# ScalarE's queue instead of SyncE's for the loads of float64 weight blocks and the stores of converted weights

## The chip, the cores and the metric

The kernel runs on one core of a Trainium2 chip. The metric is device time in microseconds for one execution. Three runs of the kernel before took 1545.47, 1546.47 and 1552.09 us, so the median is 1546.47 us. The profiled execution, from which all rows below are taken, took 1545.34 us; its span from the first to the last recorded instruction is 1543.5 us, which leaves 1.84 us around the span.

## The reference, cut to what matters

```
# q, k, v: (4, 8, 1152, 64) float32; two MLPs of d_model 512, d_ff 2048, weights float64
q_pool = q.reshape(B, H, S // 2, 2, D).mean(axis=3)          # 576 queries
scores = q_pool @ k.T / sqrt(D)
attn   = exp(scores - max) ; attn /= attn.sum() + 1e-9
x      = (attn @ v)  -> (2304, 512)
h = x @ w_in   ; x   = max(0.01 * h, h) @ w_out              # layer 0 (moe)
h = x @ w_in2  ; out = elu(h) @ w_out2                       # layer 1 (moe2)
```

Everything is computed in float32; the products of the two MLPs and of the attention are split into high and low parts, which is why most copies below come in pairs (a "hi" copy and a "lo" subtraction).

## The kernel before, in words

**Work.** Attention runs over 16 pairs of heads (4 batches, 4 pairs each). After each batch's attention its 576 rows go through the two MLPs; an MLP is 16 slices `f` of 128 hidden columns, each with an "up" product (line 629) and a "down" product (line 667). The MLPs of one batch overlap in time with the attention of the next.

**Weights.** `load_w` (line 311 on) gives slice `f` its two weight tiles `wr` of 128x512 float32, one of `w_in` and one of `w_out`. The first time a slice is used (batch 0 of each layer) the float64 words come from the input and are turned into float32 by `convert`, in blocks of 256 words: two blocks per tile, so 2 layers x 16 slices x 2 tensors x 2 blocks = 128 blocks. A block is a load into the tile `cr` (line 290), two operations on VectorE (lines 293 and 296), two on ScalarE (299 and 301), one on GpSimd (303) and a last one on VectorE that writes half of `wr` (305). `cr` has two buffers (`CB = 2`), so the load of a block has to wait until the block two before has been read by all of 293, 296, 299, 301 and 303. A finished `wr` tile is stored to DRAM as `w` (line 328, 64 stores), and the three later batches load it from there (line 323, 192 loads). From `wr`, `psplit` makes the high part on ScalarE and the low part on GpSimd (lines 261 and 267) into `wi` and `wo`; `wr` has four buffers, `wi` three and `wo` six.

**Order.** The kernel writes down each engine's instructions in an order of its own. Every operation is handed to `prog.add` with an engine, a cost in nanoseconds and a rank (a place in the wanted order); `schedule` then plays the program through with these costs: on each engine the operation with the lowest rank among those whose inputs are ready starts next. An operation's results count as ready after its end plus a latency by engine (2500 ns behind a DMA on SP). Operations are emitted in the order of the planned starts, and the engines execute them in that order, each waiting for its own inputs. All DMAs, these loads and stores too, are operations of the engine "SP" with a cost of 60 ns, and are issued from SyncE's queue, in one row with the loads of q, k and v (line 349), of `w` (323) and the stores of the output (712). A matmul of the MLPs enters the plan with 123 ns (369 for a group of three).

Of the kernel before, what the change touches and what calls it, by code (L numbers as in the profile page):

```python
# [11 lines left out]
U32 = mybir.dt.uint32  # L12
# [24 lines left out]
class Program:  # L37
# [8 lines left out]
               "PE PE": 5}  # L46

    def __init__(self):
        self.ops, self.tags = [], {}

    def buf(self, tag, bufs, make):
        used = self.tags.setdefault(tag, [])
# [1 line left out]
        used.append(b)  # L54
        return b

    def add(self, engine, cost, rank, fn, w=(), r=()):

        me = len(self.ops)
        deps, starts, frees = set(), set(), []  # L60

        def hits(accesses, part):
            return [o for o, p in accesses if p is None or part is None or p == part]

        for x in r:
            b, part = x if isinstance(x, tuple) else (x, None)
            deps.update(hits(b.writers, part))
            b.readers.append((me, part))
        for x in w:
            b, part = x if isinstance(x, tuple) else (x, None)  # L70
            deps.update(hits(b.writers, part))
            deps.update(hits(b.readers, part))
            if b.first is None:
                b.first = me
            if b.prev is not None:
                frees.append(b.prev)
            if b.before is not None:
                starts.add(b.before)
            b.writers.append((me, part))
        deps.discard(me)  # L80
        self.ops.append((engine, cost, rank, fn, deps, starts, frees))

    def schedule(self):
        ops, n = self.ops, len(self.ops)
        out = [[] for _ in range(n)]
        need = [0] * n
        for i, (_, _, _, _, deps, starts, frees) in enumerate(ops):
            d = set(deps)
            for b in frees:
                d.update(o for o, _ in b.writers + b.readers)  # L90
            d.discard(i)
            starts = {b.first for b in starts}
            for o in d:
                out[o].append((i, True))
            for o in starts - d:
                out[o].append((i, False))
            need[i] = len(d | starts)
        ready = [0.0] * n
        start = [None] * n
        idle, waiting, open_ = {}, {}, {}  # L100
        for o in ops:
            idle[o[0]] = 0.0
            waiting[o[0]], open_[o[0]] = [], []
        for i in range(n):
            if not need[i]:
                heapq.heappush(waiting[ops[i][0]], (0.0, i))
        times = [0.0]
        left = n
        while left:
            now = heapq.heappop(times)  # L110
            while times and times[0] <= now:
                heapq.heappop(times)
            again = True
            while again:
                again = False
                for e in idle:
                    while waiting[e] and waiting[e][0][0] <= now:
                        i = heapq.heappop(waiting[e])[1]
                        heapq.heappush(open_[e], (ops[i][2], i))
                    if idle[e] > now or not open_[e]:  # L120
                        continue
                    i = open_[e][0][1]
                    if e != "SP" and any(
                            t < now + self.PATIENCE * ops[i][1] and ops[o][2] < ops[i][2] - self.GAP
                            for t, o in waiting[e]):
                        continue
                    heapq.heappop(open_[e])
                    start[i] = now
                    left -= 1
                    end = idle[e] = now + ops[i][1]  # L130
                    heapq.heappush(times, end)
                    again = True
                    for o, done in out[i]:
                        e2 = ops[o][0]
                        if not done:
                            t = now
                        elif e2 == "PE" and e not in ("PE", "SP"):
                            t = end + 200
                        else:
                            t = end + self.LATENCY.get(e + " " + e2, self.LATENCY[e])  # L140
                        ready[o] = max(ready[o], t)
                        need[o] -= 1
                        if not need[o]:
                            heapq.heappush(waiting[e2], (ready[o], o))
                            heapq.heappush(times, ready[o])
        return start
# [8 lines left out]
def kernel(  # L155
# [19 lines left out]
    nc = tc.nc  # L175
    V, A, G, PE = nc.vector, nc.scalar, nc.gpsimd, nc.tensor
# [66 lines left out]
    def sb(tag, shape, dt=F32, bufs=1):  # L243
        return prog.buf(tag, bufs, lambda: sp.tile(shape, dt, tag=tag, name=tag, bufs=bufs))
# [26 lines left out]
    def convert(rank, dst, src):  # L271

        for n in range(0, 512, CW):
            r = sb("cr", [128, CW, 2], U32, CB)
            t = sb("ct", [128, CW], U32, CB)  # L280
            mag = sb("cm", [128, CW], F32, CB)

            def load(n=n, r=r):
                rv = r.ap.rearrange("p n t -> p (n t)")
                if len(src.shape) == 3:
                    k0, kn = n // src.shape[2], CW // src.shape[2]
                    rv, sv = rv.rearrange("p (c n) -> p c n", c=kn), src[:, k0:k0 + kn, :]
                else:
                    sv = src[:, n:n + CW]
                nc.sync.dma_start(out=rv, in_=sv.bitcast(U32))  # L290

            prog.add("SP", 60, rank - 1, load, w=[r])
            prog.add("DVE", dve(CW, True), rank, lambda r=r, t=t: V.tensor_scalar(  # L293
                out=t.ap, in0=r[:, :, 1], scalar1=3, scalar2=0x3FFFFFF8,
                op0=ALU.logical_shift_left, op1=ALU.bitwise_and), w=[t], r=[(r, 1)])
            prog.add("DVE", dve(CW), rank, lambda r=r, t=t: V.scalar_tensor_tensor(  # L296
                out=t.ap, in0=r[:, :, 1], scalar=0xC0000000, in1=t.ap,
                op0=ALU.bitwise_and, op1=ALU.bitwise_or), w=[t], r=[(r, 1), t])
            prog.add("ACT", act(CW, sbuf=True), rank, lambda r=r: A.activation(
                out=r[:, :, 0], in_=r[:, :, 0], func=ACTF.Copy, scale=2.0 ** -29), w=[(r, 0)], r=[(r, 0)])  # L300
            prog.add("ACT", act(CW, sbuf=True), rank, lambda r=r, mag=mag: A.activation(
                out=mag.ap, in_=r[:, :, 1].bitcast(F32), func=ACTF.Abs), w=[mag], r=[(r, 1)])
            prog.add("POOL", pool(CW), rank, lambda t=t, r=r: G.tensor_tensor(  # L303
                out=t.ap, in0=t.ap, in1=r[:, :, 0], op=ALU.add), w=[t], r=[t, (r, 0)])
            prog.add("DVE", dve(CW), rank, lambda n=n, t=t, mag=mag: V.scalar_tensor_tensor(  # L305
                out=dst[:, n:n + CW], in0=mag.ap, scalar=MIN_HI, in1=t.ap.bitcast(F32),
                op0=ALU.is_ge, op1=ALU.mult), w=[(dst, n)], r=[t, mag])
# [3 lines left out]
    def load_w(rank, layer, w_in, w_out, f):  # L311

        src = (w_in[:, f * 128:(f + 1) * 128].rearrange("(c p) f -> p c f", p=128),
               w_out[f * 128:(f + 1) * 128, :])
        rs = [sb("wr", [128, 512], F32, WRB) for _ in range(2)]
        for i, r in enumerate(rs):
            if w_in.dtype == F32:
                view = (lambda r=r: r.ap.rearrange("p (c n) -> p c n", c=DC)) if i == 0 else lambda r=r: r.ap
# [6 lines left out]
            else:  # L325
                convert(rank - CLEAD, r, src[i])
                kp = kept[layer, f, i] = Buf(lambda i=i: dram.tile([128, 512], F32, name=f"w{layer}_{f}_{i}"))
                prog.add("SP", 60, rank, lambda r=r, kp=kp: nc.sync.dma_start(out=kp.ap, in_=r.ap), w=[kp], r=[r])
        wi = sb("wi", [128, 2, DC, 128], F32R, WIB)
        wo = sb("wo", [128, 2, DM], F32R, WOB)  # L330
        psplit(rank - 0.5, WH, WL, lambda: wi[:, 0].rearrange("p c n -> p (c n)"),
               lambda: wi[:, 1].rearrange("p c n -> p (c n)"), lambda: rs[0].ap, 512, (wi, 0), [rs[0]])
        psplit(rank - 0.5, WH, WL, lambda: wo[:, 0], lambda: wo[:, 1], lambda: rs[1].ap, 512, (wo, 0), [rs[1]])
        return wi, wo


# [258 lines left out]
    def mlp(at, span, b, layer, xin, w_in, w_out, tags):  # L595
# [22 lines left out]
        def up(f):  # L618
# [4 lines left out]
            for hf in range(2):  # L623
# [7 lines left out]
                            start=(c == 0 and a == 0 and e == 0), stop=(c == DC - 1 and a == 1))  # L631

                for c in range(DC):
                    prog.add("PE", 3 * 123, rank + step * hf / 2, lambda h=h, c=c, cols=cols: mm(h, c, cols),
                             w=[h], r=[wi, (xs[c], hf), (xs[c], 2 + hf)])
                rk = rank + step * hf / 2 - HURRY
                t = sb("t1", [128, HB], F32, T1B)
# [19 lines left out]
        def down(fc):  # L657
            for hf in range(2):
                for d in range(DC):
# [10 lines left out]
                                stop=(f % FC == FC - 1 and a == 1))  # L670

                    for f in fs:
                        prog.add("PE", 3 * 123, rank, lambda f=f, mm=mm: mm(f), w=[y],
                                 r=[w[f][1], (g[f], hf), (g[f], 2 + hf)])
                    a_ = acc[d]
                    if fc == 0:
# [92 lines left out]
```

## Time and profile before

| what | kernel before |
|---|---|
| median of 3 runs (lowest, highest) | 1546.47 us (1545.47, 1552.09) |
| the profiled execution | 1545.34 us |
| its span | 1543.5 us |
| busy in the span: TensorE, VectorE | 1414.5 us (92%), 1011.4 us (66%) |
| busy in the span: ScalarE, GpSimd | 1065.9 us (69%), 830.3 us (54%) |
| mean share of the 16 DMA engines' time, queue of all tensor DMAs | 28.0% |
| chain that ended last: TensorE, VectorE, ScalarE, DMA | 64%, 21%, 6%, 3% |

In the rows, PE is TensorE, PEld its weight loads, DVE VectorE, ACT ScalarE, POOL GpSimd, and SPq the queue of SyncE. L290 is line 290 of the kernel. A row of waits names an engine that stood idle, the tile and line it was about to start, and the instruction whose end released it. The busy share is an average over stages with different limits, so the stages are looked at one by one.

### The profile page before, as it was taken

How to read it: one execution, taken by the hardware profiler on the slowest of the kernel's cores; microseconds unless marked ns; L12 is line 12 of the kernel's file. 1: busy time of each engine (PE TensorE's matmuls, PEld its weight loads, DVE VectorE, ACT ScalarE, POOL GpSimd, SP SyncE). 2: the span in 40 equal slices, each digit the busy share in tenths (PEclk: the TensorE clock that was granted, in tenths of full speed). 3: DMA queues.
4: the chain of work that ended last, by engine and by line, in shares of the span. 5: the costliest groups of instructions: out<-in, count | busy, mean ns of one | idle time of the engine just before them, and what ended most of it. 6: DMA issues, size and time to landing. Idle time of an engine off the chain costs nothing.

```text
span 1543.5 us, 28953 instructions
## 1 busy us (share of the span) xinstructions
PE 1414.5 (92%) x10288; PEld 1365.2 (88%) x10288; DVE 1011.4 (66%) x2273; ACT 1065.9 (69%) x2901; POOL 830.3 (54%) x840
## 2 busy tenths in 40 slices
PE   5878889888888898999999999999999999899997
PEld 4777788888878887999999999899999998899897
DVE  6999889899998998556565556645665554124222
ACT  6989878776678787676668776676667763443553
POOL 5443255765766667254555556254554445466662
PEclk9999999999999999999999999999999999999999
DMA  4332123343334443222222222222221121322221
GB/s 138 99 115 87 40 75 123 121 130 125 126 118 144 130 143 120 74 71 73 67 69 86 79 78 63 74 76 66 71 67 59 55 56 56 93 76 82 69 82 39
DMA packets 82642, 135.59 MB, mean 88 GB/s; under 512 B 8512, under 2 KB 26944, under 8 KB 82496
## 3 DMA queue, kind: packets, MB, share of 16 engines
q1 hardware_dynamic: 82496, 133.73, 28.0%
q8 instruction: 81, 1.33, 0.4%
q14 instruction: 65, 0.53, 0.1%
HBM read 112.20 MB, written 21.50 MB: 87 GB/s over the span
## 4 chain that ended last, share of the span: by engine, by line
PE 64%; DVE 21%; ACT 6%; issue 3%; DMA 3%; POOL 2%; SPq 0%; ACTq 0%; POOLq 0%; DVEq 0%
PE h L667 17%; PE h L629 16%; PE s L452 8%; PE o L496 7%; PE t L475 5%; DVE m L457 3%; PE s L629 3%; DVE ct L293 3%; DVE wr L305 3%; DVE ct L296 3%; DVE pt L267 2%; PE s L667 2%; PE t L373 2%; PE t L629 2%; PE t L667 2%
## 5 line engine op out<-in xcount | busy, mean ns | idle before, releaser
L667 PE MATMUL h<-g,wo 128*128 128x288 f32 x2544 | 437.1, 302 | 17.5 <-DVE t L650 7.9
L629 PE MATMUL h<-xs,wi 128*128 128x288 f32 x2520 | 429.2, 305 | 22.9 <-DVE t L650 14.2
L629 PEld LDWEIGHTS h<-xs,wi 128*128 128x128 f32 x2520 | 362.5, 190 | 32.5 <-DVE t L650 20.0
L667 PEld LDWEIGHTS h<-g,wo 128*128 128x128 f32 x2544 | 367.1, 188 | 23.8 <-DVE t L650 9.6
L457 DVE TENSOR_REDUCE m<-s 128x1 f32<-128x384 f32 x432 | 232.2, 550 | 74.4 <-PE s L452 71.6
L261 ACT ACTIVATE pt<-t 128x384 fp32r<-128x384 f32 (+1 forms) x416 | 184.0, 457 | 115.2 <-PE t L475 108.3
L463 ACT ACTIVATE p<-s,m 128x384 f32<-128x384 f32 x432 | 249.5, 588 | 18.3 <-DVE m L459 18.0
L267 DVE TENSOR_TENSOR pt<-t,pt 128x384 fp32r<-128x384 f32 (+1 forms) x416 | 206.8, 509 | 73.3 <-ACT pt L261 71.7
L267 POOL TENSOR_TENSOR g<-t,g 128x288 fp32r<-128x288 f32 x256 | 211.1, 831 | 79.9 <-ACT g L261 75.5
L267 POOL TENSOR_TENSOR wo<-wr,wo 128x512 fp32r<-128x512 f32 x128 | 166.4, 1304 | 137.5 <-ACT wo L261 134.3
L452 PE MATMUL s<-kT,qT 128*128 128x384 f32 x768 | 197.0, 354 | 25.4 <-ACT p L463 24.5
L267 POOL TENSOR_TENSOR wi<-wr,wi 128x512 fp32r<-128x512 f32 x128 | 167.6, 1309 | 91.9 <-ACT wi L261 79.3
L496 PE MATMUL o<-pt,vn 128*128 128x256 f32 (+1 forms) x1152 | 192.5, 303 | 5.5 <-DVE pt L267 3.6
L475 PE MATMUL t<-ident,p 128*128 128x128 f32 x1116 | 181.6, 277 | 12.4 <-DVE pt L267 11.7
L496 PEld LDWEIGHTS o<-pt,vn 128*128 128x128 f32 x1152 | 165.5, 190 | 10.6 <-DVE pt L267 10.2
L475 PEld LDWEIGHTS t<-ident,p 128*128 128x128 f32 x1116 | 139.4, 142 | 22.1 <-DVE pt L267 12.3
L452 PEld LDWEIGHTS s<-kT,qT 128*128 128x128 f32 x768 | 125.5, 192 | 32.2 <-ACT p L463 31.0
L303 POOL TENSOR_TENSOR ct<-ct,cr 128x256 uint32<-128x256 uint32 x128 | 98.8, 774 | 96.7 <-DVE ct L296 29.8
L261 ACT ACTIVATE g<-t 128x288 fp32r<-128x288 f32 x256 | 112.2, 445 | 49.0 <-DVE t L650 28.4
L267 POOL TENSOR_TENSOR vn<-raw,vn 128x576 fp32r<-128x576 f32 x32 | 46.4, 1449 | 174.4 <-ACT vn L261 174.4
L261 ACT ACTIVATE wo<-wr 128x512 fp32r<-128x512 f32 x128 | 80.6, 630 | 78.9 <-PE h L667 47.5
L680 DVE TENSOR_TENSOR acc<-h,acc 128x288 f32<-128x288 f32 x158 | 71.1, 452 | 67.2 <-PE h L667 66.1
(106 smaller groups left out, 2080.0 us busy)
## 6 DMA issues: line engine op xcount, KB each, us to landing
wr<-w SPq DMA_DIRECT2D x192, 256.0 KB, 2.6
cr<-in_moe_w_in_dram SPq DMA_DIRECT2D x64, 256.0 KB, 2.7
cr<-in_moe_w_out_dram SPq DMA_DIRECT2D x64, 256.0 KB, 2.7
w<-wr SPq DMA_DIRECT2D x64, 256.0 KB, 2.4
raw<-in_k_dram SPq DMA_DIRECT2D x32, 288.0 KB, 3.0
raw<-in_v_dram SPq DMA_DIRECT2D x32, 288.0 KB, 3.1
raw<-in_q_dram SPq DMA_DIRECT2D x32, 256.0 KB, 2.9
out_dram<-cr SPq DMA_DIRECT2D x16, 256.0 KB, 2.1
```

Of the source, the lines that this page charges most:

```text
L261: prog.add("ACT", act(n, sbuf=not psum), rank, lambda: A.activation(out=hi(), in_=src(), func=ACTF.Copy), w=[w], r=r)
L267: lambda: eng.tensor_tensor(out=lo(), in0=src(), in1=f32(hi()), op=ALU.subtract),
L293: prog.add("DVE", dve(CW, True), rank, lambda r=r, t=t: V.tensor_scalar(out=t.ap, in0=r[:, :, 1], scalar1=3, scalar2=0x3FFFFFF8, op0=ALU.l ...
L303: prog.add("POOL", pool(CW), rank, lambda t=t, r=r: G.tensor_tensor(out=t.ap, in0=t.ap, in1=r[:, :, 0], op=ALU.add), w=[t], r=[t, (r, 0)])
L452: PE.matmul(out=st[:, 0:384], lhsT=qa(a), rhs=kT[:, 384 * c:384 * c + 384], start=(i == 0), stop=(i == len(seq) - 1))
L457: prog.add("DVE", dve(384), rank - LR, lambda st=st, c=c: V.tensor_reduce(out=m[:, c:c + 1], in_=st[:, 0:384], axis=AX.X, op=ALU.max), w=[ ...
L463: prog.add("ACT", act(384, True), rank - LE, lambda c=c: A.activation(out=p[:, 384 * c:384 * c + 384], in_=banks[c][:, 0:384], func=ACTF.E ...
L475: PE.transpose(out=t[:, i, :], in_=p[:, (3 * c + i) * 128:(3 * c + i + 1) * 128], identity=ident)
L496: PE.matmul(out=o[:, 0:n], lhsT=vn[:, c, :], rhs=pt[th][:, a, c % 3, :], start=(c == 3 * ORDER[0] and a == 0), stop=(c == 3 * ORDER[2] + 2 ...
L629: PE.matmul(out=h[:, 0:HB], lhsT=wi[:, a, c, :], rhs=xs[c][:, e, cols], start=(c == 0 and a == 0 and e == 0), stop=(c == DC - 1 and a == 1))
L667: PE.matmul(out=y[:, 0:HB], lhsT=w[f][1][:, a, d * 128:(d + 1) * 128], rhs=g[f][:, e, cols], start=(f % FC == 0 and a == 0 and e == 0), st ...
L680: prog.add("DVE", dve(HB), rank - HURRY, lambda y=y, a_=a_, cols=cols: V.tensor_tensor(out=a_[:, cols], in0=y[:, 0:HB], in1=a_[:, cols], o ...
```

## The change

The loads of `cr` and the stores of `w` are issued by `nc.scalar` instead of `nc.sync`, and are operations of the engine "ACT" in the plan, with a cost of 80 ns. `prog.add` gets an argument `late`: so many nanoseconds after the operation's end (and the engine's latency, 155 ns for ACT) its results count as ready; both DMAs have 3000. The two stores of a slice stand behind its two `psplit`s, at rank - 0.4 instead of rank. The planned cost of a group of three MLP matmuls is 3 x 133 instead of 3 x 123 ns. The plan is worked out anew with these figures, so the order on every engine may differ. Tiles, buffers and operations are the same.

```diff
-    def add(self, engine, cost, rank, fn, w=(), r=()):
+    def add(self, engine, cost, rank, fn, w=(), r=(), late=0):
         me = len(self.ops)
+        if late:
+            self.late[me] = late
...
-                        ready[o] = max(ready[o], t)
+                        ready[o] = max(ready[o], t + self.late.get(i, 0) * done)
...
-                nc.sync.dma_start(out=rv, in_=sv.bitcast(U32))
+                nc.scalar.dma_start(out=rv, in_=sv.bitcast(U32))
...
-            prog.add("SP", 60, rank - 1, load, w=[r])
+            prog.add("ACT", 80, rank - 1, load, w=[r], late=3000)
...
-                prog.add("SP", 60, rank, lambda r=r, kp=kp: nc.sync.dma_start(out=kp.ap, in_=r.ap), w=[kp], r=[r])
+                stores.append((kp, r))
...
         psplit(rank - 0.5, WH, WL, lambda: wo[:, 0], lambda: wo[:, 1], lambda: rs[1].ap, 512, (wo, 0), [rs[1]])
+        for kp, r in stores:
+            prog.add("ACT", 80, rank - 0.4, lambda r=r, kp=kp: nc.scalar.dma_start(out=kp.ap, in_=r.ap), w=[kp], r=[r],
+                     late=3000)
...
-                    prog.add("PE", 3 * 123, rank + step * hf / 2, lambda h=h, c=c, cols=cols: mm(h, c, cols),
+                    prog.add("PE", 3 * 133, rank + step * hf / 2, lambda h=h, c=c, cols=cols: mm(h, c, cols),
...
-                        prog.add("PE", 3 * 123, rank, lambda f=f, mm=mm: mm(f), w=[y],
+                        prog.add("PE", 3 * 133, rank, lambda f=f, mm=mm: mm(f), w=[y],
```

## Rows read from the trace of the kernel before

**Rows 1.** Busy time by stage; columns: stretch, length, busy (and instructions), clock, DMA.
```profile
0.00:200.00 200.00, 153.89 (x1033) 139.33 (x1034) 171.36 (x416) 169.09 (x482) 83.73 (x93) 0.97 0.30 95
200.00:600.00 400.00, 351.26 (x2478) 328.22 (x2477) 369.48 (x790) 309.53 (x869) 257.03 (x269) 0.99 0.39 125
600.00:1543.00 943.00, 909.32 (x6781) 897.68 (x6780) 470.60 (x1068) 587.31 (x1553) 489.58 (x479) 0.99 0.24 71
```

**Rows 2.** DMA instructions of loads (L290) and stores (L328); ns min/median/max.
```profile
L290 SPq DMA_DIRECT2D cr<-in_moe_w_in_dram x64: 378/379/587, 4.7 to 578.9; - x64
L290 SPq DMA_DIRECT2D cr<-in_moe_w_out_dram x64: 327/328/579, 13.2 to 585.5; - x64
...
DMA to landing us min/median/max: 2.4/2.7/4.7
...
L328 SPq DMA_DIRECT2D w<-wr x64: 320/327/535, 25.1 to 593.9; - x64
```

**Rows 3.** The last chain after 600 us: one stretch of TensorE.
```profile
659.74 3.19 PE h L629 x24
```

**Rows 4.** DVE's waits, 200 to 600 us; total us, times, longest us.
```profile
DVE m L457 <- PE s L452: 7.5, 15, 0.9
DVE t L642 <- ACT t L640: 6.5, 4, 2.5
DVE pt L267 <- ACT pt L261: 2.9, 10, 0.5
DVE t L650 <- ACT t L648: 2.2, 3, 0.9
...
DVE ct L293 <- DMA cr<-in_moe_w_in_dram: 1.8, 3, 1.2
DVE ct L293 <- DMA cr<-in_moe_w_out_dram: 1.6, 2, 0.8
```

**Rows 5.** ACT's waits, 200 to 600 us.
```profile
ACT g L261 <- DVE t L642: 14.2, 16, 2.6
ACT g L261 <- DVE t L650: 11.9, 14, 1.8
ACT cr L299 <- DMA cr<-in_moe_w_out_dram: 11.3, 12, 2.4
...
ACT cr L299 <- DMA cr<-in_moe_w_in_dram: 2.7, 3, 1.3
```

**Rows 6.** Waits of SP's queue, 0 to 600 us.
```profile
SPq L290 <- POOL ct L303: 190.4, 116, 8.4
SPq L290 <- ACT cm L301: 72.1, 51, 4.8
SPq L328 <- DVE wr L305: 56.8, 37, 7.5
```

**Rows 7.** Instructions of one load in order of time: start us, length us.
```profile
321.35 0.75 POOL L303 TENSOR_TENSOR ct<-ct,cr 128x256 uint32<-128x256 uint32 x1 [0.95 <-ACT p L463]
...
322.12 3.32 SPq L290 DMA_DIRECT2D cr<-in_moe_w_in_dram  x2
```

**Rows 8.** ACT's groups of line 261, writing g, 200 to 600 us.
```profile
L261 ACT ACTIVATE g<-t 128x288 fp32r<-128x288 f32 x61 | 27.2, 446 | 26.5 <-DVE t L642 14.2 <-DVE t L650 11.9
```

**Rows 9.** A long conversion instruction beside one of POOL.
```profile
325.00 1.29 POOL L267 TENSOR_TENSOR wi<-wr,wi 128x512 fp32r<-128x512 f32 x1
325.07 1.50 DVE L305 SCALAR_TENSOR_TENSOR wr<-cm,ct 128x256 f32<-128x256 f32 x1
```

**Rows 10.** POOL's waits for q from DRAM, 0 to 200 and 200 to 600 us.
```profile
POOL qs L397 <- DMA raw<-in_q_dram: 14.6, 5, 4.0
...
POOL qs L397 <- DMA raw<-in_q_dram: 3.0, 3, 1.4
```

**Rows 11.** DVE's conversion groups, 200 to 600 us; busy us, mean ns, idle.
```profile
L305 DVE SCALAR_TENSOR_TENSOR wr<-cm,ct 128x256 f32<-128x256 f32 x108 | 74.8, 697 | 1.5 <-POOL ct L303 1.4
L296 DVE SCALAR_TENSOR_TENSOR ct<-cr,ct 128x256 uint32<-128x256 uint32 x106 | 69.0, 654 | 0.9
...
L293 DVE TENSOR_SCALAR ct<-cr 128x256 uint32<-128x256 uint32 x106 | 56.6, 537 | 3.6 <-DMA cr<-in_moe_w_in_dram 1.8 <-DMA cr<-in_moe_w_out_dram 1.6
```

**Rows 12.** The groups of rows 11 over the whole span; ns min/median/max.
```profile
L293 DVE TENSOR_SCALAR ct<-cr x128: 273/294/1514, 7.7 to 589.7; 128x256 uint32<-128x256 uint32 x128
L296 DVE SCALAR_TENSOR_TENSOR ct<-cr,ct x128: 403/426/1661, 9.4 to 591.1; 128x256 uint32<-128x256 uint32 x128
...
L305 DVE SCALAR_TENSOR_TENSOR wr<-cm,ct x128: 402/417/1685, 12.6 to 593.3; 128x256 f32<-128x256 f32 x128
```

More of the change, by code (lines that the diff above doesn't have):

```diff
@@ L48, in __init__ @@
     def __init__(self):
-        self.ops, self.tags = [], {}
+        self.ops, self.tags, self.late = [], {}, {}
     def buf(self, tag, bufs, make):
@@ L315, in load_w @@
         rs = [sb("wr", [128, 512], F32, WRB) for _ in range(2)]
+        stores = []
         for i, r in enumerate(rs):
```

## Prediction

> **What bounds the kernel now.** I read the busy time by stage first [rows 1], because the change touches only a part of the span: the first load of a float64 block is issued at 4.7 us and the last store at 593.9 us [rows 2]. The reader is to see three stages. From 0 to 200 us (attention of the first batch) VectorE is busy 171.4 us and ScalarE 169.1 of 200. From 200 to 600 us (104 of the 128 conversions, two MLPs, attention) VectorE is the bound: 369.5 us of 400, 92%, while ScalarE has 309.5 (77%) and TensorE 351.3. After 600 us TensorE is the bound, 909.3 of 943. In that last stage 24 matmuls take 3.19 us [rows 3], 132.9 ns each, so they run one behind the other. Nothing that moves queue is issued there.
>
> Second come the waits of VectorE in the middle stage [rows 4]. Of its 400 - 369.5 = 30.5 us of idle time the three named waits for ScalarE make 11.6, those for a block not landed 3.4, the one for TensorE's scores 7.5. Third come ScalarE's own waits [rows 5]: 26.1 us for VectorE's `t`, 14.0 us for blocks not landed, out of 90.5 us idle. Fourth, the waits of SP's queue [rows 6]: before 116 of the 128 loads SP stood waiting for GpSimd's line 303, which frees the buffer, 190.4 / 116 = 1.64 us each. [Rows 7] shows one: line 303 ends at 321.35 + 0.75 = 322.10, the load goes out at 322.12. So SP issues these loads as early as the two buffers allow, and ScalarE can hardly issue them earlier.
>
> **The change part by part.** The sum is made against the profiled execution, 1545.3 us, which is 1.1 us under the median of the runs.
>
> *Loads on ScalarE.* Each of 128 loads takes its queue 0.379 or 0.328 us [rows 2], 0.354 on average, and makes it wait until line 303 has freed the buffer; behind it stand the exponentials, copies and splits that VectorE and TensorE want next. The trace has no DMA on ScalarE, so I bound this. From below: nothing, where issue and wait fall into ScalarE's 90.5 us of idle time, or under an ACTIVATE still running. From above: every load waits as SP did and issues in the open, 1.64 + 0.35 = 2 us, 104 of them 207 us in the middle stage. That end is far, because SP came early (it had nothing else to do) and the plan puts the load on ScalarE only after line 303's planned end; what remains is the difference between plan and chip. The nearest row for a ScalarE instruction put right behind another engine's planned end is the split of `g` [rows 8]: 61 instructions, 26.5 us of idle before them, 0.43 us each, half of them with none. I take 0.43 for wait and issue together, 104 x 0.43 = 45 us of ScalarE's time in the middle stage, which brings it to 354 of 400, and 24 x 0.43 = 10 us before. What of it reaches the end? ScalarE's 90.5 us of idle cost VectorE 11.6 us of waits, 13%; the rest VectorE covers with work in hand. 55 x 0.13 = +7 us.
>
> On a wait at the head of ScalarE's queue the rows of before say nothing. The Trainium skill (Perfetto Trace Analysis, "DMA Instruction — HWDGE (DVE, Sync)" and "DVE / Act Engine Instruction") has it that an engine instruction is pushed into a wait queue and the sequencer goes on to the next, while at a DMA the sequencer itself waits for the semaphore and then writes descriptors until it is free. By this, work already pushed runs on during the load's wait, and nothing behind the load starts; no run here shows yet which of the two weighs more. If the first did, the term of +7 would be 0 and the sum -8.
>
> *Stores on ScalarE.* 64 x 0.327 = 21 us, 54 of them in the middle stage (17.7 us). They add no wait: a store stands behind the split that reads the same `wr`, and SP's wait there was for VectorE's line 305 [rows 6], which the split needs too. Bounds 0 and 17.7 us of ScalarE's time; I take half, 9 us, x 0.13 = +1. The buffer of `wr` comes free later by at most the store's place behind the split; GpSimd's low part reads the buffer for 1.29 us [rows 9] after the split anyway.
>
> *The planned landing.* The plan allowed 60 + 2500 ns from a load's start to its users, and allows 80 + 155 + 3000 now. Landing takes 2.7 us in the median and up to 4.7 [rows 2], so users stood too early in their queues. VectorE's 3.4 us [rows 4] I take as gone; ScalarE's 14.0 [rows 5] x 0.13 = 1.8. Together -5 us. Bounds: 0 (loads that leave ScalarE late eat the new margin) and -17.4. Next late behind them is the buffer itself, line 303.
>
> *SP's queue without them.* The loads of q, k, v are no longer behind the 190 us of waits. GpSimd waited 14.6 and 3.0 us for q [rows 10], but is busy only 64% of the middle stage. Bounds 0 and -17.6, I take -1.
>
> *The plan's matmul.* 133 is what the chip does [rows 3], 123 is not. After 600 us at most TensorE's idle 33.7 us are to be had [rows 1]; before, the new order can go either way. Its size shows in VectorE: lines 305, 296 and 293 take 697, 654 and 537 ns in the mean [rows 11] but 417, 426 and 294 in the median [rows 12]. The long ones stand beside a GpSimd instruction: 1.50 us from 325.07, where GpSimd runs from 325.00 to 326.29 [rows 9]. The excess is 0.280 x 108 + 0.228 x 106 + 0.243 x 106 = 80 us of the engine that bounds the stage, and which instructions meet is a matter of order. If a fifth moves, that is 16 us up or down. I take -3, for the truer plan after 600 us.
>
> Sum: +7 + 1 - 5 - 1 - 3 = -1; 1545.3 - 1 = 1544.3, said as 1544.
>
> **The rivals.**
> *ScalarE becomes the bound (slower).* If issue is never hidden, a load costs 0.43 + 0.35 = 0.78 us and a store 0.33: 104 x 0.78 + 54 x 0.33 = 99 us in the middle stage, ScalarE 309.5 + 99 = 408 of 400. It passes VectorE's 369.5 from 60 / 158 = 0.38 us per issue, and the stage itself from 90.5 / 158 = 0.57. Then the stage takes 408 plus about half of its 26.1 us of waits for VectorE, 421, so +21, less the 3 of the plan: 1563. For it: the queue is in order, and 26.1 of ScalarE's 90.5 us of idle time are waits for VectorE, which itself waits for ScalarE, so that delays come back. Against it: ScalarE is 23% idle, and VectorE rarely waits for it.
>
> *Issue and wait cost nothing (faster).* The terms +7 and +1 fall, the gains of -9 stay: 1536. For it: the ACTIVATEs of [rows 8] take 0.446 us, longer than an issue. Against it: ScalarE's 30 waits for `t` show that it is often out of work in hand. By the first half of the Trainium skill's rule above it would go this way.
>
> *The new order decides (faster).* A fifth of VectorE's 80 us of long conversion instructions goes, -16 beside the sum of -1: 1528. For it: the excess is large against everything else here. Against it: nothing in the change aims at GpSimd.
>
> *The change does little of what it says:* the loads leave at the same moment as before, since the buffers decide; this is inside my forecast.
>
> **How the numbers follow.** Forecast 0.45 (its own range 1536 to 1552), ScalarE as bound 0.25 (1552 to 1575), free issue 0.15 (1532 to 1540), order 0.15 (1518 to 1536). No change is within 0.5%, 7.7 us, which is about what a measurement of this kernel can tell: 1538.7 to 1554.2 around the median. Faster: 0.45 x 0.15 + 0.15 x 0.65 + 0.15 x 0.95 = 0.31. Slower: 0.45 x 0.07 + 0.25 x 0.88 = 0.25. Same: 0.44. For 8 in 10, I leave out a third of the order case below (0.05) and half of the ScalarE case above (0.12): 1525 to 1564.
>
> **What would show it.** ScalarE's queue holds 192 DMAs, SP's none of lines 290 and 328. Right, if VectorE's waits for ScalarE between 200 and 600 us grow from 11.6 to about 18 us, its waits for `cr` fall from 3.4 to under 1, and the last conversion ends within 5 us of its 593.3 us [rows 12]. ScalarE as bound shows as conversions that end 15 us later, with VectorE under 360 us in 400. Order shows as means of lines 293, 296 and 305 nearer their medians. The prediction is wrong if the last stage, from the end of the conversions to the end of the span, changes by more than 8 us: there I count nothing but the plan.

## The result, and the profile after

The changed kernel is slower: 1564.37 us in the median of 4 runs (1560.85 to 1566.92), against 1545.97 us (1543.60 to 1552.09, 4 runs) before, a ratio of 1.0113 with a 95% interval of 1.0083 to 1.0142. The prediction said 1544 us and no change. Its span in the profiled execution is 1559.1 us.

The stages of the changed kernel, as in [rows 1]: stretch, its length, then busy time (and instructions) of PE, PEld, DVE, ACT, POOL, the granted clock, the DMA share and GB/s.

```profile
0.00:200.00 200.00, 149.38 (x997) 134.81 (x998) 166.79 (x399) 164.10 (x466) 81.59 (x92) 0.97 0.31 92
200.00:600.00 400.00, 355.33 (x2461) 329.80 (x2459) 361.56 (x788) 309.39 (x858) 246.80 (x259) 0.98 0.39 121
600.00:1559.00 959.00, 917.23 (x6832) 902.09 (x6832) 485.61 (x1088) 594.56 (x1577) 502.01 (x491) 1.00 0.24 72
```

The reader is to see two things. ScalarE, which now issues 152 DMAs between 200 and 600 us, gets as much of its own work done there as before (busy 309.4 us against 309.5; issuing a DMA isn't counted as busy). VectorE, the engine that bounds the stage, has become emptier, 528.4 us in the first 600 us against 540.8 [rows 1]. So work reaches it later.

The loads of the changed kernel, and VectorE's last conversion instruction, as in [rows 2, 12] (ns min/median/max, first and last start in us):

```profile
L293 ACTq DMA_DIRECT2D cr<-in_moe_w_in_dram x64: 384/386/488, 0.7 to 600.6; - x64
L293 ACTq DMA_DIRECT2D cr<-in_moe_w_out_dram x64: 334/338/362, 13.1 to 607.0; - x64
...
DMA to landing us min/median/max: 2.3/2.7/5.0
...
L308 DVE SCALAR_TENSOR_TENSOR wr<-cm,ct x128: 365/522/1648, 13.1 to 613.7; 128x256 f32<-128x256 f32 x128
```

An issue takes ScalarE's sequencer 0.386 or 0.338 us, about as long as SyncE's (0.379 and 0.328 [rows 2]), and the median landing is 2.7 us on either queue. The last conversion starts at 613.7 us, 20.4 us later than before; from there to the end of the span it is 945.4 us, against 950.2 before. The time is lost before the conversions are done.

VectorE's waits of the changed kernel between 200 and 600 us, as in [rows 4]:

```profile
DVE m L465 <- PE s L460: 7.3, 14, 1.0
DVE pt L270 <- ACT pt L264: 6.2, 12, 0.9
DVE qn L266 <- PE t L381: 5.3, 3, 3.0
DVE wr L308 <- POOL ct L306: 4.4, 9, 0.8
DVE t L650 <- ACT t L648: 4.3, 4, 1.7
DVE ct L296 <- DMA cr<-in_moe_w_out_dram: 2.0, 1, 2.0
...
DVE t L658 <- ACT t L656: 1.2, 2, 0.9
```

The three waits for ScalarE sum to 11.7 us (11.6 before; I expected 18), and those for a block not landed to 2.0 (3.4 before; I expected under 1). A moved DMA that held up ScalarE so much that VectorE starved behind it would stand here, and it doesn't. VectorE's idle time in the stage grew from 30.5 to 38.4 us, and what grew are the waits for TensorE's transposes of line 381 (qn above and a smaller qxn, 6.9 us together, 0.5 before) and for GpSimd's line 306 (1.4 before, as line 303, and 4.4 now).

**Where TensorE lost it.** TensorE does the same 10288 matmuls in every version. Counted by shape up to a moment and weighted with the time from one start to the next where they run back to back (132.9 ns for 288 columns [rows 3], 174 for 384, 147 for 320, 120 for 256, 109 for the transposes but those of line 373; the 62 ns for these are an estimate, between the 59 seen most often and a median of 67), they give the work done. The time passed less that work is what TensorE has lost by then, in us:

```
by           before  changed  before's order,  changed order,  133 alone  675 ns more, SP,
                              ScalarE's queue  SyncE's queue              124 (sp_late124)
100 us         44.6     44.1       45.7            47.1           43.2         40.1
200 us         71.9     76.4       74.8            81.1           70.2         69.5
600 us        151.5    158.2      162.3           156.2          155.3        144.3
700 us        164.9    176.6      179.5           174.7          163.8        148.2
1200 us       181.2    196.8      194.7           195.2          183.0        166.2
the span's end 211.7   227.3      228.3           229.5          215.3        195.5
```

The last line is at each kernel's own end. Of the changed kernel's 15.6 us more, 11.7 are there by 700 us. "Lost" holds waits and slow stretches alike, for TensorE's granted clock has two levels in these traces, 2.4 and 1.2 GHz. Two stretches of the kernel before, both with TensorE busy throughout (columns as in [rows 1]):

```profile
1440.00:1443.00 3.00, 3.00 (x14) 3.00 (x14) 0.91 (x2) 2.78 (x7) 3.00 (x5) 0.50 0.33 87
1444.00:1447.00 3.00, 3.00 (x25) 3.00 (x24) 0.91 (x2) 2.96 (x8) 2.38 (x4) 1.00 0.37 115
```

At the lower level a matmul of 288 columns starts every 240 ns, at the upper one every 133. Over the whole span the mean is 0.990 in the kernel before and 0.989 in the changed one, so the clock is not what sets these two apart.

### The profile page after: what moved, and what is told of

It reads as the page before. It is cut to its first block, busy times and chain, and to the rows that moved or that the text cites. A ratio compares the mean times of both kernels' runs of the same rounds, so it can differ in the third digit from the quotient of the medians.

```text
span 1559.1 us, 28828 instructions
## 1 busy us (share of the span) xinstructions
PE 1421.9 (91%) x10288; PEld 1366.7 (88%) x10288; DVE 1014.0 (65%) x2273; ACT 1068.0 (69%) x2901; POOL 830.4 (53%) x840
## 4 chain that ended last, share of the span: by engine, by line
PE 59%; DVE 21%; ACT 11%; issue 4%; POOL 3%; DMA 1%; ACTq 0%; SPq 0%; POOLq 0%; DVEq 0%
PE h L675 17%; PE h L637 13%; PE s L460 7%; PE o L504 7%; PE t L483 5%; DVE m L465 3%; DVE wr L308 3%; PE s L637 3%; DVE pt L270 3%; DVE ct L299 3%; ACT p L471 2%; PE s L675 2%; DVE ct L296 2%; PE t L675 2%; PE t L381 2%
## 5 line engine op out<-in xcount | busy, mean ns | idle before, releaser
L675 PE MATMUL h<-g,wo 128*128 128x288 f32 x2544 | 445.5, 305 | 21.6 <-DVE t L658 15.5
L483 PE MATMUL t<-ident,p 128*128 128x128 f32 x1116 | 183.0, 276 | 16.9 <-DVE pt L270 10.8
L504 PEld LDWEIGHTS o<-pt,vn 128*128 128x128 f32 x1152 | 165.5, 190 | 11.7 <-DVE pt L270 11.2
```

Source lines behind the costliest of these rows:

```text
L483: PE.transpose(out=t[:, i, :], in_=p[:, (3 * c + i) * 128:(3 * c + i + 1) * 128], identity=ident)
L504: PE.matmul(out=o[:, 0:n], lhsT=vn[:, c, :], rhs=pt[th][:, a, c % 3, :], start=(c == 3 * ORDER[0] and a == 0), stop=(c == 3 * ORDER[2] + 2 ...
L675: PE.matmul(out=y[:, 0:HB], lhsT=w[f][1][:, a, d * 128:(d + 1) * 128], rhs=g[f][:, e, cols], start=(f % FC == 0 and a == 0 and e == 0), st ...
```

## The experiments

Eighteen kernels ran, each timed beside the kernel before on the same chip. A ratio is to the kernel before, with its 95% interval. What the kernel's planner does is changed in most of them, so it matters that a new plan rewrites the order on every engine.

**The queue and the order apart.** Three kernels keep one order on TensorE, VectorE, GpSimd and ScalarE's arithmetic and change the queue alone.

```diff
--- order_only: the changed kernel, its order kept
-                nc.scalar.dma_start(out=rv, in_=sv.bitcast(U32))
+                nc.sync.dma_start(out=rv, in_=sv.bitcast(U32))
...
-            prog.add(..., lambda r=r, kp=kp: nc.scalar.dma_start(out=kp.ap, in_=r.ap), ...)
+            prog.add(..., lambda r=r, kp=kp: nc.sync.dma_start(out=kp.ap, in_=r.ap), ...)
--- issue_only: the kernel before, its order kept; issue_loads: the first of the two edits alone
-                nc.sync.dma_start(out=rv, in_=sv.bitcast(U32))
+                nc.scalar.dma_start(out=rv, in_=sv.bitcast(U32))
...
-                prog.add(..., lambda r=r, kp=kp: nc.sync.dma_start(out=kp.ap, in_=r.ap), ...)
+                prog.add(..., lambda r=r, kp=kp: nc.scalar.dma_start(out=kp.ap, in_=r.ap), ...)
```

> The changed kernel with its order of instructions on TensorE, VectorE, ScalarE's compute and GpSimd kept word for word, but the 128 loads and 64 stores issued from SyncE's queue again. Theory A (the new order costs the time: conversions are placed later, because the plan holds a load's users back by 80+155+3000 ns instead of 60+2500 and puts each load at ScalarE's next free place): as slow as the changed kernel, 1558 to 1568 us, conversions ending near 612 us. Theory B (the queue costs it: loads wait in ScalarE's queue and hold ScalarE up): back at 1544 to 1550 us, conversions ending near 594 us. Something between says both.

> The kernel before with its plan and its order kept on every engine, but the 128 loads and 64 stores issued from ScalarE's queue, at the places that the plan gave them in time. Theory A (order): within 0.3% of before, 1543 to 1550 us, because an issue runs beside the ACTIVATE in work. Theory B (queue): slower by 1% or more, 1560 us or above; the stores, which wait for VectorE's line 305 there, make it worse than the changed kernel, up to 1580 us.

> The order before kept on every engine, with the 128 loads alone issued from ScalarE's queue; stores stay on SyncE. With stores it was 1560.8 us. My prediction's term of +7 us for the loads gives 1553 us here, and its +1 for stores would leave the rest of the 14.8 unexplained. If the stores, whose wait for VectorE's line 305 then stands at the head of ScalarE's queue, make the loss: 1547 to 1551 us. If the loads make all of it: 1558 to 1561 us.

| | DMAs on SyncE's queue | on ScalarE's queue |
|---|---|---|
| order before | 1 | loads 1.0050 (1.0031 to 1.0069); loads and stores 1.0099 (1.0083 to 1.0115) |
| changed order | 1.0109 (1.0087 to 1.0131) | 1.0113 (1.0083 to 1.0142) |

On the changed order the queue makes no difference that can be measured (0.04%, uncertain by some 0.4%): with all DMAs back on SyncE, the order alone loses as much as the whole change. On the order before, whose plan kept no place for them on ScalarE, loads cost 0.50% and stores another 0.49%. The two losses do not add up in the changed kernel; either one is enough.

What a DMA at the head of ScalarE's queue does is to be seen in issue_only. Rows of ScalarE in order of time, and VectorE's line 305 for which the store waits:

```profile
337.27 1.35 DVE L305 SCALAR_TENSOR_TENSOR wr<-cm,ct 128x256 f32<-128x256 f32 x1
...
337.51 0.44 ACT L261 ACTIVATE g<-t 128x288 fp32r<-128x288 f32 x1 [0.19 <-DVE t L642]
338.66 0.33 ACTq L328 DMA_DIRECT2D w<-wr  x1
339.04 0.41 ACT L640 ACTIVATE t<-h 128x288 f32<-128x288 f32 x1 [1.08 <-DVE wr L305]
```

Line 305 ends at 338.62, the store goes out at 338.66, its issue ends at 338.99, and the next ACTIVATE starts 0.05 us after that; ScalarE stood idle 1.08 us, though its next instruction wanted nothing of line 305 (the last matmul of its `h` had ended at 337.02). The other half is seen in the changed kernel, where an ACTIVATE starts while a DMA is being issued:

```profile
440.16 0.43 ACT L304 ACTIVATE cm<-cr 128x256 f32<-128x256 f32 x1
440.30 0.39 ACTq L293 DMA_DIRECT2D cr<-in_moe_w_in_dram  x1
440.49 0.43 ACT L656 ACTIVATE t<-t 128x288 f32<-128x288 f32 x1
```

The issue lasts from 440.30 to 440.69, and ScalarE computes on without a gap. Both are as the Trainium skill has it (Perfetto Trace Analysis, "DMA Instruction — HWDGE (DVE, Sync)" and "DVE / Act Engine Instruction"): what was pushed ahead of the DMA runs on, what stands behind it waits for the DMA's own wait. In issue_loads ScalarE's idle time that ended with GpSimd's line 303 (there is none in the kernel before) has these rows first, 0 to 600 us:

```profile
ACT p L463 <- POOL ct L303: 3.8, 5, 1.3
ACT pt L261 <- POOL ct L303: 2.9, 3, 1.6
ACT cr L299 <- POOL ct L303: 2.0, 3, 0.7
ACT cm L301 <- POOL ct L303: 1.7, 3, 0.6
```

With five smaller ones they make 14.4 us over 128 loads, and the kernel lost 0.50%, 7.7 us. That these waits are the 7.7 us is not shown, for the changed kernel has as many of them. There the line is 306, and its largest rows are:

```profile
ACT p L471 <- POOL ct L306: 4.9, 4, 1.5
ACT cm L304 <- POOL ct L306: 2.5, 2, 2.1
```

With seven smaller ones they make 13.7 us, against 0.4 us in order_only, and the two kernels take the same time. So the place that the new plan keeps for a load did not take its wait away. The wait is there, and in this order it costs nothing that can be measured. A store waits there as well, behind a load:

```profile
376.56 0.63 ACT L264 ACTIVATE wo<-wr 128x512 fp32r<-128x512 f32 x1
377.74 0.39 ACTq L293 DMA_DIRECT2D cr<-in_moe_w_in_dram  x1
378.31 0.92 DVE L308 SCALAR_TENSOR_TENSOR wr<-cm,ct 128x256 f32<-128x256 f32 x1
379.26 0.34 ACTq L340 DMA_DIRECT2D w<-wr  x1
379.65 0.38 ACT L515 ACTIVATE tm<-o 64x256 f32<-64x256 f32 x1 [2.46 <-DVE wr L308]
```

ScalarE is idle from 377.19 to 379.65. The load goes out when line 306 has ended (377.70) and the store when line 308 has (379.23), and the next ACTIVATE starts behind the store; its own operand `o` was complete at 378.64. The split of the tile that this store saves starts only at 382.63. Rank - 0.4 puts a store behind its split only when both are ready in the plan, and a split also needs a free buffer of `wi` or `wo`: 19 of the 64 stores of the changed kernel go out more than 1 us ahead of the split of their tile.

**The matmul's planned cost, and draws of the order.** Only the planned cost of three MLP matmuls is changed, in the kernel before (DMAs on SP) or in the changed one.

```diff
--- pe133_only, pe124, pe128: the kernel before with 133, 124, 128
-                    prog.add("PE", 3 * 123, rank + step * hf / 2, ...
+                    prog.add("PE", 3 * 133, rank + step * hf / 2, ...
...
-                        prog.add("PE", 3 * 123, rank, ...
+                        prog.add("PE", 3 * 133, rank, ...
--- after_pe123, after_pe124, after_pe128: the changed kernel with 123, 124, 128 in both places
```

> The kernel before with only the planned cost of the MLP matmuls at 3 x 133 ns; all DMAs stay on SyncE's queue. My prediction gave -3 us for it (1543). If the new order of the plan is what costs, whatever causes it, this alone may already be slower: 1552 us or more. If the late landing times of the loads in the plan cost it, this stays within 0.4% of before, 1540 to 1552 us.

> The changed kernel with the planned cost of the MLP matmuls back at 3 x 123 ns. If the matmul's cost in the plan makes the loss: 1543 to 1550 us. If loads and stores (their queue or their planned times) make it: 1558 to 1570 us.

> The kernel before with the MLP matmuls planned at 3 x 124 ns instead of 3 x 123: a step that means nothing, but which rewrites the order on every engine. Theory C (133 is worse than 123 because of what it says of TensorE): a tenth of the +6.6 us, within 0.15% of before, 1544 to 1548 us. Theory R (any other order is worse, because the one before is a lucky one among many): away from before by 0.3% or more, likely slower, 1551 to 1560 us.

> The changed kernel with the matmuls planned at 3 x 124 ns; its partner with all DMAs on SyncE is the kernel before with 124, 0.995 of before. Theory P (moving the DMAs to ScalarE in the plan has a price of its own, about what the pairs at 123 and 133 show, +0.5 to +0.7%, whichever order is drawn): 0.999 to 1.004 of before. Theory R (it is all a draw of the order): anywhere from 0.99 to 1.02.

> The kernel before with the matmuls planned at 3 x 128 ns, DMAs on SyncE: a fourth draw of the order. From 123, 124 and 133 (1, 0.995 and 1.005 of before): 0.992 to 1.008.

> The changed kernel with the matmuls planned at 3 x 128 ns: the partner of the kernel before with 128. Theory P: 0.4 to 1.2% slower than its partner, and TensorE 4 to 7 us behind it by 200 us, as in all pairs so far. Theory R: as often faster than its partner as slower.

| planned ns | DMAs planned and issued on SP | the change's loads and stores | their price |
|---|---|---|---|
| 123 | 1 | 1.0048 (1.0031 to 1.0065) | +0.48% |
| 124 | 0.9949 (0.9932 to 0.9966) | 0.9991 (0.9977 to 1.0004) | +0.42% |
| 128 | 0.9998 (0.9986 to 1.0009) | 1.0029 (1.0016 to 1.0042) | +0.31% |
| 133 | 1.0047 (1.0032 to 1.0062) | 1.0113 (1.0083 to 1.0142) | +0.66% |

A step of 1 ns in 123, which says nothing new of TensorE, makes the kernel 0.5% faster; the step to 133, where the chip is, makes it 0.5% slower. That a truer figure makes a better order has fallen: between two plans the order is close to a draw with a spread of about half a per cent either way. The pairs are what can be read: in each of four, moving the loads and stores costs 0.3 to 0.7%, on average 0.47%. In each of them the kernel with the moved DMAs also has the lower mean clock over its runs, by 0.003 to 0.004. In the 82 runs of the kernel before that were timed beside these kernels, 0.01 less of mean clock goes with about 9 us more, so by this estimate some 3 to 4 us of each price of 5 to 10 us come with the clock. Whether the order brings the lower clock was not tested.

**What in the plan makes the price.** The change gives the loads a longer planned landing, a place on ScalarE, and moves the stores. Each was tried apart.

```diff
--- late2325: the changed kernel, loads and stores planned to land after 2560 ns, as before
-... late=3000)
+... late=2325)
--- sp_late123, sp_late124: the kernel before (123, 124) with late= in add and schedule, loads on SP
-            prog.add("SP", 60, rank - 1, load, w=[r])
+            prog.add("SP", 60, rank - 1, load, w=[r], late=675)
--- loads_plan, loads_plan124: the changed kernel with 123, 124, stores as before the change
-                stores.append((kp, r))
+                prog.add("SP", 60, rank, lambda r=r, kp=kp: nc.sync.dma_start(out=kp.ap, in_=r.ap), w=[kp], r=[r])
--- order_loads124: loads_plan124, its order kept, the loads issued by nc.sync
--- loads_first, loads_first124: the changed kernel with 133, 124
-            prog.add("ACT", 80, rank - 1, load, w=[r], late=3000)
+            prog.add("ACT", 80, -1000, load, w=[r], late=3000)
```

> The changed kernel with late=2325 for loads and stores, so that the plan holds the users of a load back by 80 + 155 + 2325 = 2560 ns, as before the change. Theory L (the planned landing of 3235 ns stretches the turn of the two buffers of cr and costs the time): 1552 to 1557 us. Theory S (it is ScalarE's slot in the plan, or just another order): 1560 to 1568 us.

> The kernel before with the loads alone moved to ScalarE, in the plan (cost 80, late=3000) and on the chip; stores on SyncE, matmuls planned at 3 x 123 ns. With stores moved too it was 1553.2 us. If the loads make that half of the loss: 1551 to 1556 us. If the stores make it: 1544 to 1548 us.

> The changed kernel with the loads at rank -1000 in the plan instead of rank - 1 (31 to 38 for the first ones), so that on ScalarE a load is planned before every other operation that is ready. Theory K (on ScalarE the early loads stand behind all attention operations, whose ranks are lower, and the conversions of the first 200 us come 15 to 20 us later; that is the part of the price by 200 us): the twelfth and the eighteenth block 8 to 13 us earlier than in the changed kernel (112 and 148 us), TensorE 2 to 5 us less behind at 200 us, the whole 1553 to 1560 us. If the place of the loads does not matter: no difference by 200 us.

> The kernel before (DMAs planned and issued on SP, matmuls 3 x 123) with one change: the plan holds the users of a load back by 675 ns more, 3235 in all, as the change does. Theory L (the longer planned landing is the price of moving the loads, since a turn of cr's two buffers gets longer): 0.3 to 0.7% slower than before, TensorE 3 to 6 us more behind at 200 us. Theory S (the price is ScalarE's row in the plan): within 0.3% of before.

> The same with matmuls at 3 x 124, against its partner at 0.995 of before. Theory L: 0.998 to 1.002. Theory S: 0.992 to 0.997.

> The loads alone on ScalarE in plan and on the chip, stores on SyncE, matmuls at 3 x 124; with stores moved too it was 0.999, with none moved 0.995. At 123 the loads alone cost more (1.009) than loads and stores (1.005). If loads alone carry the price: 0.998 to 1.004. If that 1.009 was one bad draw of the order, the spread of draws is about 0.4% and this lies anywhere from 0.995 to 1.004.

> Loads and stores on ScalarE, matmuls at 3 x 124, loads at rank -1000. At 133 this gave back 0.3% of 1.1%. If the rank of the loads on ScalarE is a part of the price: 0.995 to 0.998, against 0.999 without it. If that 0.3% was a draw: 0.997 to 1.004.

> The order of the kernel with the loads alone planned on ScalarE (124, 1.0056 of before) kept word for word, the loads issued from SyncE's queue. Theory O (the place in the order makes the price, as for the whole change, where the queue made no difference): 1.003 to 1.008. Theory Q (the queue makes it): 0.989 to 0.996, where the loads on SP with the longer landing and without it lie.

| kernel | ratio | against | difference |
|---|---|---|---|
| late2325 | 1.0180 (1.0157 to 1.0203) | changed, 1.0113 | +0.7% |
| sp_late123 | 0.9936 (0.9913 to 0.9960) | before, 1 | -0.6% |
| sp_late124 | 0.9907 (0.9885 to 0.9929) | pe124, 0.9949 | -0.4% |
| loads_plan | 1.0087 (1.0066 to 1.0108) | before, 1 | +0.9% |
| loads_plan124 | 1.0056 (1.0033 to 1.0079) | pe124, 0.9949 | +1.1% |
| order_loads124 | 1.0017 (0.9998 to 1.0036) | sp_late124, 0.9907 | +1.1% |
| loads_first | 1.0080 (1.0062 to 1.0097) | changed, 1.0113 | -0.3% |
| loads_first124 | 1.0100 (1.0078 to 1.0122) | after_pe124, 0.9991 | +1.1% |

*The longer planned landing helps.* I had thought it the price (a longer turn of the two buffers); it is a gain of 0.4 to 0.6%, and taking it away from the changed kernel costs 0.7%. Each of the three lies near the spread of a draw, but all go one way. The waits for a block not landed go with them, 0 to 600 us: VectorE's were 10.9 us in pe124 and are 0.8 us in sp_late124 (first two rows pe124, then sp_late124, columns as in [rows 4]), and 5.0 us in the changed kernel became 11.0 in late2325. That these waits alone make the gain is likely but not shown.

```profile
DVE ct L293 <- DMA cr<-in_moe_w_in_dram: 10.7, 9, 5.9
...
DVE ct L293 <- DMA cr<-in_moe_w_out_dram: 0.2, 1, 0.2
...
ACT cr L302 <- DMA cr<-in_moe_w_in_dram: 7.3, 8, 3.5
...
DVE ct L296 <- DMA cr<-in_moe_w_in_dram: 0.8, 1, 0.8
```

The stages of sp_late124 show VectorE fuller and the whole shorter:

```profile
0.00:200.00 200.00, 151.56 (x1051) 136.97 (x1052) 177.65 (x421) 170.00 (x487) 84.68 (x94) 1.00 0.30 95
200.00:600.00 400.00, 355.96 (x2521) 334.20 (x2521) 370.00 (x807) 318.14 (x888) 261.78 (x275) 0.98 0.40 126
600.00:1527.00 927.00, 899.62 (x6720) 887.28 (x6719) 459.11 (x1047) 577.74 (x1528) 482.33 (x473) 1.00 0.24 71
```

VectorE is busy 547.7 us of the first 600, against 540.8 before and 528.4 in the changed kernel.

*The loads' place on ScalarE costs 1.1% in the plan.* sp_late124 and order_loads124 have the same queue, the same planned landing (3235 ns) and the same stores; in the one the loads stand in the plan as SP's operations, in the other as ScalarE's. The second is 1.1% slower, and its VectorE is emptier:

```profile
0.00:200.00 200.00, 149.10 (x965) 134.67 (x966) 164.36 (x395) 160.16 (x456) 80.04 (x90) 0.95 0.29 92
200.00:600.00 400.00, 357.69 (x2510) 337.40 (x2509) 361.90 (x794) 311.10 (x876) 246.25 (x258) 0.97 0.38 119
```

526.3 us in the first 600. ScalarE's queue then adds 0.4% (loads_plan124, 1.0056 against 1.0017, intervals that just overlap), here in a plan that kept a place for each load. At 123 the two together come to the same 1.5% (1.0087 against 0.9936 of sp_late123). Part of the 1.1% goes with the clock: in the two profiled runs the mean is 0.979 and 0.993, some 44 us more at the lower level, which would cost at most 20 of their 23 us if TensorE had work all that time; by the means over all runs (0.983 and 0.990) and the 9 us per 0.01 above it is about 7 of 17 us. Both are estimates. Moving the stores beside the loads gives some back: 1.0087 to 1.0048 at 123, 1.0056 to 0.9991 at 124.

*It is not the loads' rank.* In the plan ScalarE takes the lowest rank first, and the first loads' ranks (31 and more) stand behind all attention of the first batch; GpSimd's line 303 of the 13th block starts at 111.7 us in the changed kernel and at 87.8 before. With rank -1000 it starts at 95.8, but TensorE had lost 77.3 us by 200 us, no less than the 76.4 of the changed kernel, and the whole was once 0.3% faster and once 1.1% slower. What in ScalarE's row of the plan spoils the order stays open.

**A version that beats both.** The longer landing, loads on SP, stores on ScalarE, 124:

```diff
--- best124: sp_late124 with the change's stores
+        for kp, r in stores:
+            prog.add("ACT", 80, rank - 0.4, lambda r=r, kp=kp: nc.scalar.dma_start(out=kp.ap, in_=r.ap), w=[kp], r=[r],
+                     late=3000)
```

> A version put together from the parts: loads planned and issued on SP with 675 ns more of planned landing, stores on ScalarE behind the splits as in the change (cost 80, late=3000), matmuls at 3 x 124. Loads on SP with the longer landing alone gave 0.991 of before. Beside loads on ScalarE, moving the stores gave 0.4% (at 123) and 0.65% (at 124) back. If parts add up: 0.984 to 0.988. If the stores only make good for what loads on ScalarE spoil: 0.989 to 0.995.

It measured 0.9916 (0.9892 to 0.9941): faster than both kernels, and no better than sp_late124, 0.9907, 1529.78 us in the median. Moving the stores gave something back only beside loads on ScalarE. Seven of these nine kernels (late2325, both sp_late, both loads_plan, loads_first124, order_loads124) came out outside every range that I had written for them: I could foresee little of a new plan's time.

## Why the prediction was wrong, point by point

The step that failed is the last term of the sum, "the plan's matmul", -3 us "for the truer plan after 600 us", and beside it a term that the sum did not have: what it costs the order when the loads and stores are planned on ScalarE. I bounded what an order is worth with 16 us either way and then took a value near 0 with the wrong sign. The order alone is worth +1.09% here, 16.9 us: as much as the whole measured loss and more than all my other terms together. Of it the planned 133 ns alone measured +0.47%, about 7 us, where I had -3, and the rest, 0.6%, comes with the loads and stores. By 600 us TensorE had lost 6.7 us more than before, by 700 us 11.7, and only some 4 after that: not in the late stage for which I had meant the term. Why a plan with the loads on ScalarE makes the worse order stays open.

- *Loads on ScalarE, +7.* On the order before, 0.50% of 1546 us, 7.7 us: the size came out by luck. The idle time behind line 303 is 14.4 us, where I had 55 for wait and issue together, and I let 13% of it through. On the changed order the term is 0 within some 0.4%, though the same waits are there (13.7 us); at 124, with the loads alone, the queue adds 0.4%. What such a wait costs depends on the order around it, and one factor for all of it was no measure.
- *Stores, +1.* 0.49%, 7.6 us, on the order before, where the store stands at the head of ScalarE's queue waiting for line 305. In the changed kernel my reason (a store stands behind the split that reads the same `wr`) fails for 19 of 64 stores, and one of them is seen to wait. What that costs was not measured apart; beside moved loads the time even fell by 0.4 to 0.65% when the stores moved too, in a new plan each time.
- *The planned landing, -5.* The sign was right and the size too small: alone it is worth 0.6 and 0.4%, 9.9 and 6.5 us. VectorE's waits for blocks were counted from 200 us on (3.4 us), and the first 200 us had 7 more; in the changed kernel 5.0 of the 10.5 us are left.
- *SP's queue, -1.* Not measured apart. No run speaks for more.
- *ScalarE as the bound* gave 1563 us, the time that came, and two of its signs came or nearly came: conversions 15 us later (20.4) and VectorE under 360 us in 400 (361.6). It is still wrong, for with the DMAs taken from ScalarE's queue the kernel stays as slow (order_only). The order makes the same signs; a rival can have the time and the signs and not the cause.
- *Free issue* has the queue's price on the changed order right, but not the reason: an ACTIVATE does run beside an issue, but the waits are not free of idle time. It was useless for the time.
- *The order decides* was the right cause with the wrong sign. I let it go one way only, since "nothing in the change aims at GpSimd"; but a plan worked out anew has no reason to be better. VectorE's long conversion instructions, by which I sized it, are indeed those beside GpSimd's (81 of the 128 of line 305 overlap one and take 805 ns in the mean, the other 47 take 412), but they don't carry it: up to 640 us the three lines together take 235.6 us before and 231.9 in the changed kernel. What grew is the time in which VectorE and TensorE wait.
- *The last stage,* from the last conversion to the end, changed by 5 us, within the 8 that I had allowed.

## What to carry to other kernels

Where a program orders its own instructions by a plan, moving an operation to another engine is first of all a new plan: keep the old order and change the queue alone, keep the new order and change it back, and compare, before any engine is charged with the loss. Draw the plan a few times with a figure that means nothing changed by 1%; a gain or loss inside that spread (half a per cent here) is not yet the change's, and only pairs tell. A DMA at the head of a compute engine's queue holds back what stands behind it until its own wait is over. What that costs has to be measured in the order at hand: here some 14 us of such waits went with 0.5% in one order and with nothing measurable in another. And a landing planned too early makes the engine behind it wait in order.

## What the runs showed that I had not expected

One nanosecond in 123 of a planned cost moved the time by 0.5%, and 675 ns in the planned landing of 128 loads by 0.4 to 0.6%, with no tile, operation or queue changed: ratios of 0.9907 and 1.0113 are 2.1% apart, between kernels that execute the same instructions but for the queue of 192 DMAs. ScalarE's issue of a DMA takes about as long as SyncE's (0.386 and 0.338 us against 0.379 and 0.328), and beside ACTIVATEs already under way it can leave no gap (440.30 to 440.69).
